# First chunk of an attention and MoE kernel: part of an exponential moved to GpSimd, a cast moved to VectorE, filler products on TensorE, and the order of the weight conversion

## The chip, the cores and the metric

One core of a Trainium2 chip. The metric is device time in microseconds (us) of one execution, the median of several runs. Engines: TensorE (PE in the rows, its weight loads PEld), VectorE (DVE), ScalarE (ACT), GpSimd (POOL), and SyncE (SP), which issues the DMAs.

## What is computed

Eight sequences of 576 tokens, eight heads of 64. Heads 0 to 3 look at a local band, heads 4 to 7 at every 32nd token; the outputs go through a two-layer network with squared ReLU.

```python
def _attn_ref(q, k, v):                 # (8, 8, 576, 64)
    scores = (1.0 / np.sqrt(D)) * np.matmul(q, k.transpose(0, 1, 3, 2))
    rel = pos[:, None] - pos[None, :]
    mask_local = (rel >= 0) & (rel < 32)                                     # heads 0..3
    mask_strided = (rel >= 0) & (pos[None, :] % 32 == pos[:, None] % 32)     # heads 4..7
    scores = np.where(masks, scores, -1e9)
    attn = np.exp(scores - np.max(scores, axis=-1, keepdims=True))
    attn = attn / (np.sum(attn, axis=-1, keepdims=True) + 1e-09)
    return np.matmul(attn, v)

def _moe_ref(x, w_in, w_out):           # x 4608 x 512, w_in 512 x 2048, w_out 2048 x 512
    h = np.maximum(x @ w_in, 0.0)
    return h * h @ w_out
```

The network's weights come in double precision and the products are made from a high and a low part of each operand (hi x hi, hi x lo, lo x hi), kept in the type `F32R`.

## The kernel before, in words

The 4608 tokens are cut into 12 chunks of 384. For each chunk and each of 16 blocks of 128 features, `up` makes 12 products of 128x384 (line 475) and squares the ReLU, and `down` makes 9 products of 128x512 (line 508) into three banks that hold the output. The main loop's step s runs `up(s)` and `down(s-2)`. TensorE works on nearly nothing else, while the other engines prepare the attention of the next chunk.

Only the first chunk has nothing to hide behind. Before its first `up` it needs

- `first[0]` and `first[1]`: the two pairs of local heads, and `late[0]` and `late[1]`: the two pairs of strided heads, all run by the generator `pe_pair`: scores on TensorE (L325), mask and row minimum on VectorE (L330), exponential on ScalarE (L353, four per head with bias and row sum, for the local pairs; for the strided pairs one per head, L356, after a subtraction on GpSimd, L355), row sums and reciprocal on VectorE (L357 to L359), division (L362, on VectorE for local and GpSimd for strided pairs), transposes on TensorE (L368) with copies out of PSUM (L370 on VectorE, L372 on ScalarE), the product with v (L380 local, L391 strided), and the split into high and low part (L395, L396);
- the weights of the first blocks, which `convert` makes from the raw 64-bit numbers: a rescaling on ScalarE (L154, one per block of weights), then for each half a step on ScalarE (L166), one on VectorE (L169), the high part on ScalarE (L172) and the low part on GpSimd (L173). `convert` goes on through the whole first chunk, one block a step.

In the first chunk `up` ends with ReLU on ScalarE (L483), the square on VectorE (L484), the high part `gh` on ScalarE (L488) and the low part `gl` on VectorE (L489). `gh` and `gl` have two buffers each, so those of block j wait for the products of block j-2.

The order on each engine is made by the tile framework: it takes the program's order as priority and lets an instruction go ahead when, by its own plan of the times, it is ready first. `tc.issue_after(i)` holds the instructions of a block behind i on i's engine alone; `behind` does so for a generator, with one instruction for each engine. A queue, once made, runs strictly in its order. `zeros(bank, n)` makes n products of 128x128 that nobody reads (L605); L503 and the tripled L380 of `first[0]` are of this kind too. The main program (L607 to L650) names the order of the prologue: the scores, 45 filler products, the exponentials of `first[0]` and of the first head of `first[1]`, the scores of `late[1]`, `late[0]`'s exponentials, `first[0]`'s transposes, the exponentials of `first[1]`'s second head, its transposes, `late[1]`'s exponentials, two steps of weights, and so on.

Of the kernel before, what the change touches and what calls it, by code (L numbers as in the profile page):

```python
# [11 lines left out]
AF = mybir.ActivationFunctionType  # L12
ALU = mybir.AluOpType
AX = mybir.AxisListType
# [14 lines left out]
QC = 96  # L29
NW = TC // QC  # L30
# [8 lines left out]
NWARM = 60  # L39
# [10 lines left out]
def f32(ap):  # L50
    return ap.bitcast(F32)
# [11 lines left out]
def windows(c):  # L63

    res, at = [], 0
    for b, g in SEGS[c]:
        for qc in (2 * g, 2 * g + 1):
            if res and res[-1][:2] != (b, qc - 1):
                at += STR
            res.append((b, qc, at))  # L70
            at += QC
    return res
# [14 lines left out]
def attn_moe(ctx: ExitStack, tc, qk_l, v_l, qk_d, v_d, qk_p, v_p, f_s, q_s, k_s, v_s, w_in, w_out, masks, eye, out):  # L87
    nc = tc.nc
# [13 lines left out]
    def psum(i, nm):  # L102

        return ps.tile([P, 512], F32, name=nm, tag=f"ps{i}")
# [17 lines left out]
    last = {}  # L122
# [9 lines left out]
    def fetch(k):  # L132

        p, which = order[k]
        src = (w_out if which else w_in)[p].bitcast(U32).rearrange("p (n t) -> p n t", t=2)
        if k < 12:
            raw = wpool.tile([P, 1024, 2], U32, name=f"raw{k}", tag=f"w{k + 8 if k < 8 else k + 4}")
            nc.sync.dma_start(out=raw, in_=src)
            raws[k] = [(raw, slice(0, 1024))]
        else:  # L140
            raws[k] = []
            for i in range(0, 1024, WP):
                raw = spool.tile([P, WP, 2], U32, name=f"raw{k}_{i}", tag="s3", bufs=5)
                nc.sync.dma_start(out=raw, in_=src[:, i : i + WP])
                raws[k].append((raw, slice(i, i + WP)))

    def convert():

        split = None

        def scale(k):
            for raw, _ in raws[k]:

                nc.scalar.activation(f32(raw[:, :, 1]), f32(raw[:, :, 1]), AF.Prelu, scale=2.0**-112, alpha=-(2.0**32))  # L154

        scale(0)
        for k in range(NFT):
            p, which = order[k]
            t = wpool.tile([P, 2, 1024], F32R, name=f"w{which}_{p}", tag=f"w{k}")
            (wo if which else wi)[p] = t[:, 0], t[:, 1]  # L160
            cuts = [(raw[:, i : i + WP], sl.start + i) for raw, sl in raws.pop(k) for i in range(0, sl.stop - sl.start, WP)]
            for raw, at in cuts:

                z = psum(zbank[next(zturn) % len(zbank)], f"z{k}_{at}").bitcast(U32)
                w, hi, lo = raw[:, :, 1], t[:, 0, at : at + WP], t[:, 1, at : at + WP]
                first_step = nc.scalar.activation(z, raw[:, :, 0], AF.Copy, bias=-0.49, scale=2.0**-29 * (1 - 2.0**-9))  # L166
                if split:
                    split()
                last["v"] = nc.vector.scalar_tensor_tensor(out=w, in0=w, scalar=3, in1=z, op0=ALU.logical_shift_left, op1=ALU.bitwise_or)  # L169

                def split(w=w, hi=hi, lo=lo, at=at, k=k):
                    last["a"] = nc.scalar.copy(hi, f32(w))  # L172
                    last["g"] = nc.gpsimd.tensor_sub(lo, f32(w), f32(hi))  # L173
                    if at and 4 <= k < 12:
                        fetch(k + 4)

                if k == 0 and at:
                    split()
                    split = None
                if not at and k + 1 < NFT and k + 1 in raws:  # L180
                    with tc.issue_after(first_step.ins):
                        scale(k + 1)
                yield
        split()
# [110 lines left out]
    def pe_pair(c, pr, local, qk, vr, es, pt, banks, sm, single):  # L295
# [3 lines left out]
        if local:  # L299
            kw, wins, nv = KW, [at for _, _, at in windows(c)], P  # L300
            src, vsrc = qk_d[c, pr], v_d[c, pr]
            mk = [mask_sb[:QC, w % 2, :] for w in range(NW)]
        else:
            kw, wins, nv = QC, [QC * w for w in range(NW)], QC
# [9 lines left out]
        nm = small.tile([P, 2, NW], F32, name=f"nm{u}", tag="nm")  # L314
        rs = small.tile([P, 2, NW], F32, name=f"rs{u}", tag="rs")
        ss = sums[sm]
# [3 lines left out]
        e4 = [blocks(e) for e in es]  # L320

        r4 = [blocks(t) for t in s_ps] if single else e4
# [23 lines left out]
                minima(h, s)  # L346
        yield
        for h in range(2):
            if single:
                for w in range(NW):  # L350
                    if c == 0 and pr and h and not w:
                        yield
                    last["a"] = nc.scalar.activation(r4[h][:, w], e4[h][:, w], AF.Exp, bias=nm[:QC, h, w : w + 1], scale=-1.0, accum_out=ss[:QC, NW * h + w, :1])  # L353
            else:
                nc.gpsimd.tensor_sub(e4[h], e4[h], nm[:QC, h].unsqueeze(2).broadcast_to([QC, NW, kw]))  # L355
                last["a"] = nc.scalar.activation(e4[h], e4[h], AF.Exp, scale=-1.0)  # L356
                nc.vector.tensor_reduce(out=ss[:QC, NW * h : NW * (h + 1), 0], in_=e4[h], op=ALU.add, axis=AX.X)  # L357
        nc.vector.tensor_reduce(out=rs[:QC].rearrange("p h w -> p (h w)"), in_=ss[:QC], op=ALU.add, axis=AX.X)
        last["v"] = nc.vector.reciprocal(rs[:QC], rs[:QC])  # L359
# [4 lines left out]
        p4 = pt.rearrange("p (h w q) -> p h w q", h=2, w=NW)  # L364
        for h in range(2):
            t = s_ps[h] if s_ps else banks()
            for w in range(NW):
                nc.tensor.transpose(t[:kw, w * QC : (w + 1) * QC], e4[h][:, w], ident[:QC, :QC])  # L368
            if c == 0 and not local:
                nc.vector.tensor_copy(pt[:kw, h * TC : (h + 1) * TC], t[:kw, :TC])  # L370
            else:
                last["a"] = nc.scalar.copy(pt[:kw, h * TC : (h + 1) * TC], t[:kw, :TC])  # L372
# [92 lines left out]
    def up(c, j):  # L465
        x = xt[c]
        p, o = divmod(j, 2)
        ph = psum((c * NFT + j) % 3, f"h{c}_{j}")
        n = 0
        for kt in range(4):  # L470
            kind, kk = "ls"[kt // 2], kt % 2
            xh, xl = x[kind, "h"][:, kk, :], x[kind, "l"][:, kk, :]
            wsl = slice(kt * 256 + o * P, kt * 256 + (o + 1) * P)
            for w, xx in ((wi[p][0], xh), (wi[p][0], xl), (wi[p][1], xh)):
                done = nc.tensor.matmul(ph[:, :TC], w[:, wsl], xx, start=n == 0, stop=n == 11)  # L475
                n += 1
        gh = gpool.tile([P, TC], F32R, name=f"gh{c}_{j}", tag="gh")
        gl = gpool.tile([P, TC], F32R, name=f"gl{c}_{j}", tag="gl")
        g = ph[:, :TC]
        if c == 0:  # L480

            r = p_t[j % 2].rearrange("p w q -> p (w q)")
            nc.scalar.activation(r, g, AF.Relu)  # L483
            nc.vector.scalar_tensor_tensor(out=g, in0=g, scalar=0.0, in1=r, op0=ALU.max, op1=ALU.mult)  # L484
        else:
            nc.scalar.activation(g, g, AF.Relu)  # L486
            nc.scalar.activation(g, g, AF.Square)  # L487
        last["gh"] = nc.scalar.copy(gh, g)  # L488
        nc.vector.tensor_sub(gl, g, f32(gh))  # L489
        g_tiles[c, j] = gh, gl  # L490
        return done
# [29 lines left out]
    def behind(ins, gen):  # L521

        while True:
            with ExitStack() as st:
                for i in ins.values():
                    st.enter_context(tc.issue_after(i.ins))
                try:
                    k = next(gen)
                except StopIteration:
                    return  # L530
            yield k
# [47 lines left out]
    def take(c, which):  # L579

        if NPLAIN <= c < NCHUNK:
            for h in map(int, which):
                if (c, h) not in heads:
                    heads[c, h] = pe_head(c, h)
                with ExitStack() as st:
# [4 lines left out]
                    last["pe"] = last.get("mm", last["pe"])  # L590

    ungated = convert()

    late = [pair_at(0, pr, False, 2 + pr, ("y0", "14")[pr]) for pr in range(2)]
# [7 lines left out]
    def zeros(bank, n):  # L602
        w_ps = psum(bank, f"w_ps{bank}")
        for _ in range(n):
            nc.tensor.matmul(w_ps[:, :P], warm, warm, start=True, stop=True)  # L605
# [17 lines left out]
        for k in range(NEARLY, 8):  # L623
            fetch(k)
    next(late[0])
    zeros(1, 3 * NWARM // 4)
    next(first[0])
    parts = last["v"], last["a"]
    with tc.issue_after(parts[1].ins):
# [4 lines left out]
    next(first[0])  # L634
    with tc.issue_after(last["a"].ins):
        next(first[1])
    weights = behind({"a": last["a"]}, ungated)
    next(first[1])
    next(late[1])
    for _ in range(2):  # L640
        next(weights)
    next(first[0])
# [4 lines left out]
    weights = behind({"a": last["a"]}, ungated)  # L647
# [6 lines left out]
    for s in range(NS + 2):  # L654
        c, j = divmod(s, NFT)
# [19 lines left out]
        if s < NFT - 2:  # L675

            weights = behind({"a": last["gh"]} | ({"x": last["xs"]} if s > NFT - 4 else {}), ungated)
# [108 lines left out]
```

## Time and profile before

| what | us |
|---|---|
| median of 3 runs | 880.89 (880.71 to 881.8) |
| the profiled execution | 881.58 |
| its span, first to last instruction | 879.80 |
| TensorE busy in the span | 869.2 |
| ScalarE, VectorE, GpSimd busy | 571.7, 640.5, 672.4 |

All times in the rows are counted from the span's start. The profiled execution took 1.78 us more than its span, and 0.69 us more than the median. TensorE's "busy" is a union of overlapping products: an `up` product is listed with some 0.33 us and a `down` product with 0.39 us, but the next one begins about 0.17 and 0.23 us later.

### The profile page before, as it was taken

The numbers are of one execution on the slowest core, as the hardware profiler recorded it, in microseconds if no ns is written. First come the engines' busy times: TensorE is split into PE (matmuls) and PEld (weight loads), VectorE is DVE, ScalarE is ACT, GpSimd is POOL, SyncE is SP. The second block draws the span as 40 slices with busy tenths as digits, with TensorE's granted clock in tenths as the row PEclk, the third lists the DMA queues.
The fourth block names the chain that finished last, engine by engine and source line by source line (L and its number), as shares of the span: only waits on it lengthen the run. The fifth ranks groups of instructions, "written<-read, shape, count | busy, mean of one in ns | idle before, by whom it ended". The sixth has DMA issues, their size and how long they took to land.

```text
span 879.8 us, 14906 instructions
## 1 busy us (share of the span) xinstructions
PE 869.2 (99%) x4773; PEld 790.0 (90%) x4773; DVE 640.5 (73%) x1900; ACT 571.7 (65%) x1506; POOL 672.4 (76%) x718
## 2 busy tenths in 40 slices
PE   8999999999999999999999999999999999999997
PEld 7788899999999999999999999999998989999996
DVE  5796687787787887878878778878787787883111
ACT  6999777586676566657657758657666665664332
POOL 3589778877988989888988978997998899782000
PEclk9999999999999999999999999999999999999999
DMA  9853531323123023112202302312131121000000
GB/s 356 356 199 107 163 101 39 101 84 113 31 78 111 26 89 103 44 51 85 67 13 80 115 13 74 97 38 75 31 102 57 32 71 61 6 1 12 26 1 36
DMA packets 26798, 71.41 MB, mean 81 GB/s; under 512 B 2976, under 2 KB 8736, under 8 KB 25184
## 3 DMA queue, kind: packets, MB, share of 16 engines
q1 hardware_dynamic: 26432, 70.14, 24.0%
q8 instruction: 37, 0.61, 0.3%
q14 instruction: 41, 0.34, 0.1%
q10 hardware_dynamic: 288, 0.33, 0.1%
HBM read 61.01 MB, written 9.44 MB: 80 GB/s over the span
## 4 chain that ended last, share of the span: by engine, by line
PE 90%; POOL 4%; ACT 2%; DVE 1%; DMA 1%; issue 1%; DVEq 0%; POOLq 0%; ACTq 0%
PE y L508 42%; PE h L475 42%; POOL w L173 2%; PE s L237 2%; PE o L283 2%; DMA raw<-w_out 1%; PE w_ps L605 1%; PE b L380 1%; ACT b L353 1%; ACT raw L154 1%; ACT z L166 0%; POOL pp L447 0%; DVE sc L432 0%; PE b L391 0%; POOL e L355 0%
## 5 line engine op out<-in xcount | busy, mean ns | idle before, releaser
L508 PE MATMUL y<-w,gh 128*128 128x512 f32 x1152 | 357.9, 391 | 0.5 <-POOL w L173 0.5
L508 PEld LDWEIGHTS y<-w,gh 128*128 128x128 f32 x1152 | 212.7, 188 | 40.5 <-POOL w L173 0.8
L475 PE MATMUL h<-xlh,w 128*128 128x384 f32 x768 | 229.1, 339 | 1.4 <-ACT xlh L395 0.9
L447 POOL TENSOR_TENSOR pp<-vs,sc 128x448 f32<-128x448 f32 (+10 forms) x192 | 189.9, 1013 | 48.9 <-DVE qs L448 23.0
L475 PE MATMUL h<-xsh,w 128*128 128x384 f32 x768 | 226.3, 335 | 0.3 <-POOL w L173 0.3
L508 PE MATMUL y<-w,gl 128*128 128x512 f32 x576 | 225.2, 392 | 0.0
L425 POOL TENSOR_TENSOR pq<-ks,qs 128x512 f32<-128x512 f32 (+2 forms) x192 | 197.7, 1050 | 18.6 <-DVE sc L426 13.2
L489 DVE TENSOR_TENSOR gl<-h,gh 128x384 fp32r<-128x384 f32 x192 | 105.5, 550 | 80.9 <-ACT gh L488 79.6
L488 ACT CAST gh<-h 128x384 fp32r<-128x384 f32 x192 | 91.3, 476 | 104.4 <-PE y L508 103.0
L486 ACT ACTIVATE h<-h 128x384 f32<-128x384 f32 x176 | 83.1, 472 | 110.0 <-PE h L475 109.5
L426 DVE TENSOR_REDUCE sc<-pq 128x8 f32<-128x512 f32 (+4 forms) x228 | 119.7, 534 | 45.3 <-POOL pq L425 42.6
L475 PEld LDWEIGHTS h<-xlh,w 128*128 128x128 f32 x768 | 141.3, 188 | 5.0 <-ACT xlh L395 1.1
L475 PEld LDWEIGHTS h<-xsh,w 128*128 128x128 f32 x768 | 141.4, 188 | 1.1 <-POOL w L173 0.6
L475 PE MATMUL h<-xll,w 128*128 128x384 f32 x384 | 129.0, 336 | 0.0
L508 PEld LDWEIGHTS y<-w,gl 128*128 128x128 f32 x576 | 108.1, 188 | 22.9
L475 PE MATMUL h<-xsl,w 128*128 128x384 f32 x384 | 128.3, 334 | 0.0
L448 DVE TENSOR_REDUCE qs<-pp 128x64 f32<-128x448 f32 (+11 forms) x192 | 106.4, 562 | 27.2 <-POOL pp L447 25.2
L487 ACT ACTIVATE h<-h 128x384 f32<-128x384 f32 x176 | 83.2, 473 | 3.6
L262 DVE STREAM_TRANSPOSE p_t<-e 32x128 f32<-32x128 f32 x240 | 72.3, 301 | 11.2 <-ACT e L251 6.6
L475 PEld LDWEIGHTS h<-xll,w 128*128 128x128 f32 x384 | 72.2, 188 | 2.4 <-DVE xll L396 0.3
L475 PEld LDWEIGHTS h<-xsl,w 128*128 128x128 f32 x384 | 72.1, 188 | 0.1
L246 ACT ACTIVATE e<-e,nm 96x128 f32<-96x128 f32 x160 | 62.5, 392 | 10.0 <-DVE nm L229 8.7
(101 smaller groups left out, 1077.2 us busy)
## 6 DMA issues: line engine op xcount, KB each, us to landing
qk<-qk_l SPq DMA_DIRECT2D x24, 400.0 KB, 3.2
y<-ysb SPq DMA_DIRECT2D x36, 256.0 KB, 3.5
raw<-w_in SPq DMA_DIRECT2D x7, 1024.0 KB, 10.9
qk<-qk_l SPq DMA_DIRECT2D x16, 416.0 KB, 3.2
vs<-v_s SPq DMA_DIRECT2D x10, 576.0 KB, 3.8
raw<-w_out SPq DMA_DIRECT2D x5, 1024.0 KB, 12.6
v<-v_l SPq DMA_DIRECT2D x40, 128.0 KB, 2.0
ks<-k_s SPq DMA_DIRECT2D x8, 576.0 KB, 3.7
```

Of the source, the lines that this page charges most:

```text
L246: nc.scalar.activation(e[:QC, cut(w)], e[:QC, cut(w)], AF.Exp, bias=nmax[:QC, w : w + 1], scale=-1.0, accum_out=ssum[:QC, w, :1])
L262: nc.vector.transpose(out=pt[STR * k : STR * (k + 1), :, STR * r : STR * (r + 1)], in_=e.rearrange("p (w k) -> p w k", k=KW)[STR * r : STR ...
L425: nc.gpsimd.tensor_mul(pv, kt[:, a : a + m, :], qt[:, i - i0 : i - i0 + 1, :].broadcast_to([P, m, D]))
L426: nc.vector.tensor_reduce(out=sc[:, i - i0, a : a + m], in_=pv, op=ALU.add, axis=AX.X)
L447: nc.gpsimd.tensor_mul(pv, vt[:, a : a + nd, :n], sc[:, il : il + 1, :n].broadcast_to([P, nd, n]))
L448: nc.vector.tensor_reduce(out=ot[:, il, a : a + nd], in_=pv, op=ALU.add, axis=AX.X)
L475: done = nc.tensor.matmul(ph[:, :TC], w[:, wsl], xx, start=n == 0, stop=n == 11)
L486: nc.scalar.activation(g, g, AF.Relu)
L487: nc.scalar.activation(g, g, AF.Square)
L488: last["gh"] = nc.scalar.copy(gh, g)
L489: nc.vector.tensor_sub(gl, g, f32(gh))
L508: done = nc.tensor.matmul(y_ps[c][t], g[:, sl], w[:, wsl], start=j == 0 and k == 0, stop=j == NFT - 1 and k == 2)
```

## The change

Five edits, all for the first chunk:

1. `first[1]`'s second head: its four exponentials with bias and row sum become a subtraction on GpSimd, one exponential over 96x512 on ScalarE and one row sum on VectorE.
2. More filler on TensorE: `zeros(1, ...)` makes 55 products in place of 45, and the four transposes of `first[0]`'s second head are made twice.
3. `convert` gives up control once more, after its first rescaling, and that first rescaling is called right behind `first[1]`'s exponentials, ahead of `first[1]`'s transposes and `late[1]`'s exponentials.
4. The first two steps of weights are held behind the first exponential of `late[1]` on ScalarE (`last["a0"]`) and behind its reciprocal on VectorE, in place of behind the last exponential of `first[1]` on ScalarE.
5. In `up` of the first chunk ScalarE makes the ReLU twice and no longer makes `gh`; VectorE makes the square twice, first into `gh`, then in place. The weights of a step are held behind the second ReLU, where they were held behind the copy to `gh`.

```diff
@@ convert @@
         scale(0)
+        yield
@@ pe_pair @@
         for h in range(2):
-            if single:
+            if single and pr and h:
+                yield
+                nc.gpsimd.tensor_sub(e4[h], e4[h], nm[:QC, h].unsqueeze(2).broadcast_to([QC, NW, kw]))
+                last["a"] = nc.scalar.activation(r4[h], e4[h], AF.Exp, scale=-1.0)
+                nc.vector.tensor_reduce(out=ss[:QC, NW * h : NW * (h + 1), 0], in_=r4[h], op=ALU.add, axis=AX.X)
+            elif single:
                 for w in range(NW):
-                    if c == 0 and pr and h and not w:
-                        yield
                     last["a"] = nc.scalar.activation(r4[h][:, w], e4[h][:, w], AF.Exp, bias=nm[:QC, h, w : w + 1], scale=-1.0, accum_out=ss[:QC, NW * h + w, :1])
             else:
...
+                last["a0"] = last["a0" if h else "a"]
...
-            for w in range(NW):
+            for w in [*range(NW)] * (2 if c == 0 and local and not pr and h else 1):
                 nc.tensor.transpose(t[:kw, w * QC : (w + 1) * QC], e4[h][:, w], ident[:QC, :QC])
@@ up @@
             nc.scalar.activation(r, g, AF.Relu)
-            nc.vector.scalar_tensor_tensor(out=g, in0=g, scalar=0.0, in1=r, op0=ALU.max, op1=ALU.mult)
+            last["gh"] = nc.scalar.activation(r, g, AF.Relu)
+            for t in (gh, g):
+                nc.vector.scalar_tensor_tensor(out=t, in0=g, scalar=0.0, in1=r, op0=ALU.max, op1=ALU.mult)
         else:
             nc.scalar.activation(g, g, AF.Relu)
             nc.scalar.activation(g, g, AF.Square)
-        last["gh"] = nc.scalar.copy(gh, g)
+            last["gh"] = nc.scalar.copy(gh, g)
@@ the main program @@
-    zeros(1, 3 * NWARM // 4)
+    zeros(1, NWARM - 5)
...
-    weights = behind({"a": last["a"]}, ungated)
+    next(behind({"a": last["a"]}, ungated))
     next(first[1])
     next(late[1])
+    weights = behind({"a": last["a0"], "v": last["v"]}, ungated)
```

## Rows read from the trace of the kernel before

**Rows 1.** The page, first part: busy us, share of the span, instructions.

```profile
PE 869.2 (99%) x4773; PEld 790.0 (90%) x4773; DVE 640.5 (73%) x1900; ACT 571.7 (65%) x1506; POOL 672.4 (76%) x718
```

**Rows 2.** Waits of TensorE, 27.5 to 110 us: waiter <- releaser: total us, times, longest.

```profile
PE h L475 <- ACT xlh L395: 0.9, 1, 0.9
PE s L237 <- POOL qx L223: 0.5, 1, 0.5
PE y L508 <- POOL w L173: 0.5, 1, 0.5
PE h L475 <- ACT w L172: 0.4, 1, 0.4
PE h L475 <- POOL w L173: 0.3, 1, 0.3
```

**Rows 3.** Stretches: length, PE, PEld, DVE, ACT, POOL busy (instructions), clock, DMA, GB/s.

```profile
13.10:16.50 3.40, 2.28 (x26) 1.62 (x25) 3.33 (x18) 3.33 (x14) 1.50 (x3) 1.00 1.01 419
16.50:20.00 3.50, 3.50 (x46) 3.50 (x44) 2.57 (x17) 3.13 (x11) 2.88 (x4) 0.51 1.01 417
20.00:23.40 3.40, 2.94 (x30) 2.20 (x29) 2.70 (x5) 2.91 (x6) 1.61 (x2) 1.00 1.01 412
...
42.00:57.00 15.00, 14.88 (x77) 13.29 (x78) 13.47 (x32) 14.31 (x26) 11.75 (x13) 1.00 0.40 143
```

**Rows 4.** The same for the transposes of L368 alone: length, PE, PEld, clock, DMA.

```profile
20.00:23.40 3.40, 2.54 (x24) 2.03 (x24) 1.00 1.01 412
```

**Rows 5.** TensorE in order of time: start, us, operation, [idle before <- releaser].

```profile
9.86 2.69 PE L605 MATMUL w_ps<-p_t 128*128 128x128 bf16 x45
...
14.42 1.17 PE L368 MATMUL b<-ident,e 96*128 96x96 f32 x8 [0.62 <-ACT b L353]
15.97 4.22 PE L380 MATMUL b<-pt,v 128*64 128x96 f32 x48 [0.38 <-ACT pt L372]
...
27.50 0.45 PE L475 MATMUL h<-xlh,w 128*128 128x384 f32 x1
...
88.03 0.88 PE L380 MATMUL b<-pt,v 128*64 128x96 f32 x16
```

**Rows 6.** ScalarE in order of time.

```profile
15.46 0.83 ACT L372 COPY pt<-b 128x384 f32<-128x384 f32 x2
...
18.77 0.35 ACT L353 ACTIVATE b<-e,nm 96x128 f32<-96x128 f32 x1
19.16 1.11 ACT L154 ACTIVATE raw<-raw 128x1024 f32<-128x1024 f32 x1
...
60.16 0.63 ACT L356 ACTIVATE e<-e 96x512 f32<-96x512 f32 x1
```

**Rows 7.** VectorE in order of time.

```profile
21.17 1.27 DVE L362 TENSOR_TENSOR e<-b,rs 96x512 f32<-96x512 f32 x2
...
61.26 0.67 DVE L357 TENSOR_REDUCE sums<-e 96x4 f32<-96x512 f32 x1
```

**Rows 8.** GpSimd in order of time.

```profile
20.03 1.61 POOL L362 TENSOR_TENSOR w<-w,rs 96x384 f32<-96x384 f32 x2 [0.30 <-DVE rs L359]
24.88 1.30 POOL L173 TENSOR_TENSOR w<-raw,w 128x512 fp32r<-128x512 f32 x1 [3.25 <-ACT w L172]
...
58.08 1.03 POOL L355 TENSOR_TENSOR e<-e,nm 96x512 f32<-96x512 f32 x1
```

**Rows 9.** DMA issues from 6.0 to 6.4 us: KB, us from issue to landing.

```profile
raw<-w_in SPq DMA_DIRECT2D x1, 1024.0 KB, 8.8
```

**Rows 10.** Groups by line, 27 to 108 us: busy us, mean ns | idle before, releasers.

```profile
L484 DVE SCALAR_TENSOR_TENSOR h<-h,p_t 128x384 f32<-128x384 f32 x16 | 9.0, 561 | 5.4 <-ACT p_t L483 5.3
L489 DVE TENSOR_TENSOR gl<-h,gh 128x384 fp32r<-128x384 f32 x16 | 8.8, 547 | 3.1 <-ACT gh L488 3.0
...
L483 ACT ACTIVATE p_t<-h 128x384 f32<-128x384 f32 x16 | 7.7, 479 | 1.1 <-PE h L475 1.1
L488 ACT CAST gh<-h 128x384 fp32r<-128x384 f32 x16 | 7.5, 469 | 1.4 <-PE y L508 0.9 <-DVE h L484 0.4
```

## The prediction

> **What bounds the kernel now.** The page comes first: TensorE is busy for 869.2 of 879.8 us [rows 1], so only its idle time and its slow time can be won. The list of its waits shows where that is: from the first product of `up` at 27.50 us [rows 5] to 110 us there are five waits with 2.6 us in all [rows 2], and behind them the products follow each other without a gap. What is left is the 27.50 us ahead of `up`, and its order of time shows two weak places. Between the scores and the transposes of `first[0]` TensorE is idle for 0.62 us, and 0.38 us more before the 48 products with v [rows 5]. And in the stretch 13.1 to 16.5, where it is busy for 2.28 of 3.40 us, the granted clock is 1.00, but in the next, 16.5 to 20.0, it is 0.51, the lower of its two levels (1.2 and 2.4 GHz) [rows 3]. The 48 products take 4.22 us there, 0.088 us each; at full clock 16 of them take 0.88 us, 0.055 each [rows 5].
>
> **The prologue: the second head of `first[1]`.** Four exponentials, each followed by a read of the row sum, go from ScalarE; the last begins at 18.77 and ends at 19.16, when the rescaling begins, so one takes 0.39 us [rows 6]. They were interleaved with `late[1]`'s. In their place comes one exponential of 96x512, 0.63 us, issued behind the copies of `first[0]` that take 15.46 to 16.29 [rows 6]. Those copies wait for the doubled transposes: four more at 0.11 us (24 take 2.54 [rows 4]) are 0.43 us, of which the first copy covers some 0.2, so the exponential runs from about 16.5 to 17.1. Its input is ready: the subtraction is 1.03 us on GpSimd [rows 8], which has nothing to do before the strided pairs' minima are made, and VectorE makes this head's ahead of them; `late[0]`'s subtractions, queued behind it, come some 0.3 us later, and ScalarE is then still at `first[1]`'s first head, so that costs nothing (0.3 if not). VectorE gets a row sum more, 0.67 us [rows 7], and the work queued behind it there is `late[1]`'s row sums. The division L362 of `first[1]`, which began at 21.17 [rows 7], can begin near 18.6, 2.5 us earlier.
>
> `late[1]` gains nothing. The first rescaling (1.11 us [rows 6]) is now ahead of its exponentials on ScalarE; its data was issued just after 6.0 us and landed 8.8 us later, before 15 [rows 9], so nothing blocks, but `late[1]`'s first exponential moves back by up to that. And `first[1]`'s division (1.27) stands ahead of `late[1]`'s sums on VectorE. Its division on GpSimd, 20.03 to 21.64 [rows 8], moves by -0.3 to +1.2 us; I take +0.8. From its end to the first `up` now go 5.9 us, part of it in TensorE's queue behind the products of `first[1]`, which then are done; the chain itself (transposes, VectorE copies, L391, ScalarE casts) is some 4 us. So `late[1]` lets `up` begin at 22.4 + 3.5 = 25.9, the last products of L391 lying beside the first six of `up`, which need only local heads.
>
> **The prologue: TensorE.** Ten filler products at 2.69 / 45 = 0.06 us [rows 5] push the scores of `late[1]` by 0.6 us, into the 0.62 us wait: nothing. The doubled transposes fill the second gap and start the 48 products at 16.4 in place of 15.97, 0.4 us later. If the clock stays up they take 48 x 0.055 = 2.64 us and end at 19.0, not 20.19: 1.15 us won. From there to 27.50 TensorE has 7.3 us of work and waits, of which 0.6 us or so are waits for `first[1]`'s and `late[0]`'s copies. So `up` could begin between 25.7 (waits gone) and 26.4 (waits kept). With `late[1]`'s 25.9 I take 26.0: **-1.5 us**.
>
> A page speaks against the doubled transposes. The Trainium skill (TensorE: Matmul & The Clock Gate, "Part 4: PE-mode transpose") says that a transpose on TensorE does not count as busy, for the clock, in the way a product does. By that the 48 products would again run at the lower level, and the sum would be near that of the second rival. The trace disagrees: from 20.0 to 23.4 us transposes are 2.54 of TensorE's 2.94 us [rows 3, 4], and the clock stays at 1.00.
>
> **The weights.** The first low part starts at 24.88 on GpSimd [rows 8], 2.6 us before the product at 27.50; `up` needs it by its third product. With the rescaling some 2 us earlier and VectorE's step let go behind `late[1]`'s reciprocal (about 20.5 to 21) both halves come about 2 us earlier, so they do not set the start at 26.0. The next blocks set three of the five waits: 0.5 + 0.4 + 0.3 [rows 2]. ScalarE is full there; it saves 4 x 0.39 - 0.63 = 0.9 us of exponentials, and of its idle time between 16.5 and 23.4 us, 0.9 us [rows 3], some can go. So the conversion moves by 0.9 to 1.8 us, about as much as `up`, and the three waits stay: 0, between +0.4 and -0.6.
>
> **The sixteen steps.** ScalarE: a ReLU (479 ns) for a cast (469) [rows 10]: 16 x 0.01 = 0.2 us, nothing. VectorE: one square more. The write to `gh` in this form is not in the trace; the nearest rows have the same inputs, one from PSUM and one from SBUF, with output to PSUM (561 ns) and to SBUF (547) [rows 10], begun some 0.47 us apart. 16 x 0.47 = 7.5 us. Against it VectorE no longer waits for ScalarE's cast: 3.0 us [rows 10]. Net 4.5 us, over 80 us; in the whole span VectorE is idle for a quarter [rows 1]. The wait of `gh` for the products of two blocks before moves from ScalarE (0.9 us [rows 10]) to VectorE, with the conversion's L169 queued behind. I take 0 for TensorE here; the ends are -1.4 (below) and +4.5 (no cover).
>
> At the end of the chunk TensorE waits 0.9 and 0.5 us [rows 2] for work that VectorE and GpSimd finish last. Some of VectorE's 3.0 us behind the cast [rows 10] lie there; between 0 and the whole 1.4 I take **-0.3 us**.
>
> **Sum.** -1.5 - 0.3 = -1.8 us: the span 879.8 becomes 878.0, this execution 881.58 becomes 879.8, and the median, 0.69 us below that execution, 879.1. A measurement of this kernel tells about 0.2%, 1.76 us, from no change; the forecast is just at that bound.
>
> **Rivals.**
> - More than forecast (15%): with `gh` no longer crossing engines the wait at the chunk's end goes whole, and half of the three early ones: -1.5 - 1.4 - 0.6 = -3.5, 877.4. For it: VectorE's 3.0 us of waits [rows 10] lie in the queue that feeds everything. Against: GpSimd is nearly full later in the chunk, and is given nothing back.
> - The start comes earlier but is swallowed (27%): either the clock falls all the same (10%), or the conversion (17%), whose engines have no room, pins TensorE at the next blocks. With the clock down the 48 products, begun at 16.4, end where they ended or later; what stays is the waits of 0.6 less 0.3: 880.6. The pinned case gives the same: the waits of [rows 2] grow by what the start gained. For it: weights come up to a microsecond ahead of use, no more; against: ScalarE saves 0.9 us at the front.
> - Slower (18%): VectorE becomes the bound. From 42 to 57 us it is busy for 13.47 of 15 us [rows 3]; 3.6 steps at 0.47 add 1.7, which makes 15.2. From there on each step's L169 comes later, and with it the high part and GpSimd's low part, and TensorE waits for weights. It decides when VectorE's net addition (4.5 us) finds no idle time that the others don't need. Price: 4.5 less the 1.8 won, half a microsecond for what is covered: +2.2, 883.1.
> - The edits do what they say in all of these; the framework may order the queues otherwise than I read, which widens each case by half a microsecond.
>
> **How the numbers follow.** Forecast 879.1 with 40%, its own range 878.1 to 880.1. Faster than 879.13: a little over half of it and rival one, a bit from the second: 0.40. Slower than 882.65: 0.16. Same: 0.44. The range 876.9 to 882.7 takes in the forecast, the swallowed case, most of the first rival and the near edge of the slow one.
>
> **What would show it.** Clock at 1.00 from 16.5 to 20 and 48 products in 2.6 us; the first product of `up` near 26.0 in place of 27.50; `first[1]`'s division near 18.6; no wait of VectorE for `gh`; the three early waits for weights unchanged at about 1.2 us. Wrong if the clock is still 0.5 there, if TensorE gains waits for L172 or L173 between 42 and 100 us, if VectorE has no idle time left there, or if the waits after 100 us grow by what the start gained.

## The result, and the profile after

The changed kernel takes 884.58 us (median of 6, 883.02 to 885.84) against 880.80 (6 runs) for the kernel before: ratio 1.0043, 95% interval 1.0033 to 1.0054. It is slower by 3.8 us where 1.8 us less was forecast, and outside the range. The profiled execution took 884.37 us with a span of 882.6. The clock is not what was lost: the four executions with a mean granted clock of 0.999 or 1.000 took 883.85 to 884.79 us.

The page's first part for the changed kernel, which answers [rows 1]: TensorE's busy time is the same, so what was lost is waiting.

```profile
PE 869.2 (98%) x4787; PEld 789.5 (89%) x4787; DVE 647.9 (73%) x1917; ACT 571.2 (65%) x1499; POOL 673.9 (76%) x719
```

The changed kernel's lines bear other numbers: `up` is L482, `down` L517, the division L368, the squares L493, `gl` L498. Stretches as in [rows 3]:

```profile
16.50:20.00 3.50, 2.98 (x53) 2.41 (x52) 3.40 (x18) 3.50 (x7) 3.18 (x4) 1.00 1.02 421
...
42.00:57.00 15.00, 15.00 (x79) 13.32 (x78) 13.65 (x38) 14.97 (x28) 12.46 (x13) 1.00 0.49 152
```

The clock stays at 1.00 from 16.5 to 20 us, where it was 0.51. TensorE in order of time, answering [rows 5]: the 48 products take 0.38 + 2.19 us in place of 4.22, but the first `up` is at 28.12 us in place of 27.50, behind two waits for copies of `late[1]`.

```profile
16.31 0.38 PE L387 MATMUL b<-pt,v 128*64 128x96 f32 x2
16.95 2.19 PE L387 MATMUL b<-pt,v 128*64 128x96 f32 x46 [0.26 <-ACT pt L379]
...
25.76 0.35 PE L398 MATMUL b<-w,v 96*32 96x96 f32 x2 [0.32 <-DVE w L377]
26.68 1.51 PE L398 MATMUL b<-w,v 96*32 96x96 f32 x30 [0.57 <-DVE w L377]
28.12 0.44 PE L482 MATMUL h<-xlh,w 128*128 128x384 f32 x1
```

What made `late[1]` late stands in three queues. ScalarE (b is `first[1]`, w is `late[1]`):

```profile
16.79 0.60 ACT L354 ACTIVATE b<-e 96x512 f32<-96x512 f32 x1
17.32 1.19 ACT L154 ACTIVATE raw<-raw 128x1024 f32<-128x1024 f32 x1
18.39 0.94 ACT L361 ACTIVATE w<-w 96x384 f32<-96x384 f32 x2
```

VectorE: the division of `first[1]` (L368), `late[1]`'s sums (L363), then copies and a split of the other pairs ahead of the last two steps that `late[1]` needs (L364, L365):

```profile
18.58 1.28 DVE L368 TENSOR_TENSOR e<-b,rs 96x512 f32<-96x512 f32 x2
19.78 1.00 DVE L363 TENSOR_REDUCE sums<-w 96x4 f32<-96x384 f32 x2
20.70 1.01 DVE L377 COPY pt<-b 96x384 f32<-96x384 f32 x2
21.63 0.15 DVE L364 TENSOR_REDUCE rs<-sums 96x8 f32<-96x16 f32 x1
21.71 0.54 DVE L403 TENSOR_TENSOR xll<-b,xlh 128x384 fp32r<-128x384 f32 x1
22.17 0.19 DVE L365 RECIPROCAL rs<-rs 96x8 f32<-96x8 f32 x1
```

GpSimd, which had the division of `late[1]` at 20.03 before [rows 8]:

```profile
22.50 1.61 POOL L368 TENSOR_TENSOR w<-w,rs 96x384 f32<-96x384 f32 x2 [2.62 <-DVE rs L365]
```

The loss at the first `up` is 0.6 us; at the first product of the third chunk it is 2.6 (176.49 against 173.90). The 2.0 us between are all lost before TensorE's product L238, which waits for `qx`: it begins at 110.56 us, 82.4 behind the first `up`, where the same product L237 of the kernel before begins at 107.92, 80.4 behind. From there to the end of the span it is 772.0 us against 771.9. That is 2.8 us between the two spans; the medians differ by 3.8, since the kernel before was profiled in one of its slower executions (881.58 us). TensorE's waits from 27.5 to 112 us make 4.2 us, against 2.6 in [rows 2]; the old wait for `xlh` and three for weights are gone or smaller, new ones are `gh`, `gl` and `xll`, and the wait for `qx` grew from 0.5:

```profile
PE s L238 <- POOL qx L224: 1.5, 1, 1.5
PE y L517 <- DVE gh L493: 1.0, 1, 1.0
PE b L375 <- DVE xll L403: 0.6, 1, 0.6
PE y L517 <- DVE gl L498: 0.6, 1, 0.6
PE y L517 <- POOL w L174: 0.5, 1, 0.5
```

Groups from 27 to 108 us, answering [rows 10]: the square to `gh` takes 548 ns, and VectorE's wait of 3.0 us for ScalarE's cast is gone (0.1 us before `gl`).

```profile
L493 DVE SCALAR_TENSOR_TENSOR h<-h,p_t 128x384 f32<-128x384 f32 x16 | 8.8, 553 | 0.0
L493 DVE SCALAR_TENSOR_TENSOR gh<-h,p_t 128x384 fp32r<-128x384 f32 x16 | 8.8, 548 | 1.1 <-ACT p_t L491 0.9
L498 DVE TENSOR_TENSOR gl<-h,gh 128x384 fp32r<-128x384 f32 x16 | 8.7, 548 | 0.1
...
L490 ACT ACTIVATE p_t<-h 128x384 f32<-128x384 f32 x16 | 7.8, 488 | 1.4 <-PE h L482 1.4
```

The waits for `gh` and `gl` stand at the first `down`, where the buffers are still free. There the second ReLU (L491) of block 0 comes 1.9 us behind the first (L490) on ScalarE, and `gh` waits for it; `gl` then waits on VectorE behind two steps of the weights. ScalarE, VectorE and TensorE:

```profile
33.95 0.49 ACT L490 ACTIVATE p_t<-h 128x384 f32<-128x384 f32 x1
...
35.85 0.47 ACT L491 ACTIVATE p_t<-h 128x384 f32<-128x384 f32 x1
```

```profile
36.35 0.56 DVE L493 SCALAR_TENSOR_TENSOR gh<-h,p_t 128x384 fp32r<-128x384 f32 x1 [0.67 <-ACT p_t L491]
```

```profile
36.96 1.66 PE L517 MATMUL y<-w,gh 128*128 128x512 f32 x6 [0.97 <-DVE gh L493]
```

One more line stands out. VectorE's subtraction L439, which takes 0.55 us at its second place in the kernel before, took 3.84 us here; at its first place it is the other way about, 3.29 us at 47.07 us before and 0.72 us at 46.92 us here. First VectorE, then GpSimd, late in the chunk:

```profile
89.47 3.84 DVE L439 TENSOR_TENSOR sc<-sc,mx 128x36 f32<-128x36 f32 x1
93.23 0.55 DVE L403 TENSOR_TENSOR xll<-b,xlh 128x384 fp32r<-128x384 f32 x1
```

```profile
88.12 5.13 POOL L174 TENSOR_TENSOR w<-raw,w 128x512 fp32r<-128x512 f32 x4
```

It ends when GpSimd's four low parts end, and `xll`, for which TensorE waits 0.6 us, is queued behind it.

### The profile page after: what moved, and what is told of

Its sections match the earlier page's. It is cut to its first block, busy times and chain, and to the rows that moved or that the text cites. A ratio compares the mean times of both kernels' runs of the same rounds, so it can differ in the third digit from the quotient of the medians.

```text
span 882.6 us, 14941 instructions
## 1 busy us (share of the span) xinstructions
PE 869.2 (98%) x4787; PEld 789.5 (89%) x4787; DVE 647.9 (73%) x1917; ACT 571.2 (65%) x1499; POOL 673.9 (76%) x719
## 4 chain that ended last, share of the span: by engine, by line
PE 94%; ACT 2%; DVE 2%; POOL 1%; issue 1%; DVEq 0%; POOLq 0%; ACTq 0%
PE h L482 44%; PE y L517 44%; PE s L238 2%; PE o L284 2%; PE w_ps L614 1%; PE b L326 1%; ACT b L358 1%; ACT z L167 1%; DVE sc L439 0%; ACT w L173 0%; PE b L398 0%; DVE raw L170 0%; ACT raw L154 0%; PE b L375 0%; ACT p_t L490 0%
## 5 line engine op out<-in xcount | busy, mean ns | idle before, releaser
L517 PE MATMUL y<-w,gh 128*128 128x512 f32 x1152 | 356.8, 391 | 1.6 <-DVE gh L493 1.0
L517 PEld LDWEIGHTS y<-w,gh 128*128 128x128 f32 x1152 | 212.5, 188 | 42.4 <-POOL w L174 1.2
L482 PE MATMUL h<-xlh,w 128*128 128x384 f32 x768 | 228.7, 338 | 0.0
L482 PE MATMUL h<-xsh,w 128*128 128x384 f32 x768 | 226.2, 335 | 0.1
L517 PE MATMUL y<-w,gl 128*128 128x512 f32 x576 | 223.8, 392 | 0.6 <-DVE gl L498 0.6
L498 DVE TENSOR_TENSOR gl<-h,gh 128x384 fp32r<-128x384 f32 x192 | 105.4, 549 | 82.1 <-ACT gh L497 80.8
L497 ACT CAST gh<-h 128x384 fp32r<-128x384 f32 x176 | 83.9, 476 | 104.8 <-PE y L517 103.7
L482 PEld LDWEIGHTS h<-xlh,w 128*128 128x128 f32 x768 | 141.4, 188 | 3.2 <-POOL w L174 0.4
L482 PEld LDWEIGHTS h<-xsh,w 128*128 128x128 f32 x768 | 141.2, 188 | 0.6 <-POOL w L174 0.4
L517 PEld LDWEIGHTS y<-w,gl 128*128 128x128 f32 x576 | 108.0, 188 | 23.8 <-DVE gl L498 1.0
L482 PE MATMUL h<-xll,w 128*128 128x384 f32 x384 | 129.0, 336 | 0.0
L482 PE MATMUL h<-xsl,w 128*128 128x384 f32 x384 | 128.3, 334 | 0.0
L482 PEld LDWEIGHTS h<-xll,w 128*128 128x128 f32 x384 | 72.2, 188 | 2.2
L482 PEld LDWEIGHTS h<-xsl,w 128*128 128x128 f32 x384 | 72.1, 188 | 0.0
```

Of the source, the lines that this page charges most:

```text
L517: done = nc.tensor.matmul(y_ps[c][t], g[:, sl], w[:, wsl], start=j == 0 and k == 0, stop=j == NFT - 1 and k == 2)
```

## The experiments

Medians; the ratio's 95% interval is against the kernel before on the same chip (its medians there: 880.64 to 880.90).

| run | us | ratio |
|---|---|---|
| e1: before + edit 5 | 882.34 | 1.0013 to 1.0032 |
| e2: changed, edit 5 undone | 882.89 | 1.0019 to 1.0038 |
| e3: changed, one ReLU | 884.49 | 1.0029 to 1.0059 |
| e4: changed, edits 3 and 4 undone | 884.29 | 1.0024 to 1.0054 |
| e5: before + edit 1 | 882.28 | 1.0009 to 1.0030 |
| e6: before + edit 2 | 880.05 | 0.9986 to 1.0006 |
| e7: before + edits 3, 4 | 882.27 | 1.0010 to 1.0028 |
| e8: changed, one subtraction on GpSimd | 886.45 | 1.0058 to 1.0088 |
| e9: before + 1, 2, `late[1]` first, held | 884.41 | 1.0021 to 1.0052 |
| e10: before + a square of no use | 881.17 | 0.9995 to 1.0021 |
| e11: e9 without the hold | 883.46 | 1.0018 to 1.0039 |
| e12: e11 + edit 5 | 885.56 | 1.0023 to 1.0058 |
| f1: before + 2, 5 | 881.49 | 0.9998 to 1.0016 |
| f2: before + 2 + a square of no use | 880.46 | 0.9987 to 1.0016 |
| f3: before + 2, weights held behind ReLU | 880.75 | 0.9992 to 1.0011 |
| f4: before + 2, cast on VectorE | 879.85 | 0.9979 to 0.9998 |
| f5: before + 2, 5 with one ReLU | 882.09 | 1.0008 to 1.0027 |
| f6: changed, f4's form in place of edit 5 | 881.47 | 1.0001 to 1.0019 |

**The edits one by one: e1, e5, e6, e7, and e2.** Each takes its edits from the diff, word for word.

> The kernel before with edit 5 alone (two ReLUs on ScalarE, two squares on VectorE, no cast). Theory A, the steps cost: VectorE's 16 more squares and the late second ReLU make gh late and the end of the chunk late; the first product of up stays at 27.5 us, the second chunk's first up comes 1.5 to 3 us later, median 882.5 to 884. Theory B, the prologue costs and all else is carried along: within 0.7 us of before, 880.3 to 881.5.

> The changed kernel with edit 5 taken back: edits 1 to 4 alone. Theory A: the first product of up stays near 28.1 us, 0.6 later than before, the rest of the chunk goes as before, median 881 to 882. Theory B: the delay of the second strided pair's division (22.5 against 20.0 us) pushes the whole chunk, median 883.5 to 885.

> The kernel before with edit 1 alone (second head of the second local pair by a GpSimd subtraction and one exponential). If the local pair's earlier division, now ahead of the strided pair's row sums on VectorE, is what delays that pair: its division begins 8 us or more behind the first local division (6.4 in the kernel before), up starts no earlier, 881.5 to 883. If edit 1 does what I forecast: division at 6.4 to 7.5, up 1 us earlier, 879.5 to 880.6.

> The kernel before with edit 2 alone (55 filler products, four transposes twice). If filler only keeps the clock up: 1.00 throughout the prologue, the first up about 12.9 us behind the first local division in place of 13.9, 879.8 to 880.8. If it costs: the later minima of the last strided pair push its division beyond 7 us behind the first local division, 881.5 to 882.5.

> The kernel before with edits 3 and 4 alone (first rescaling early, the first weights behind the strided pair's reciprocal). If the rescaling ahead of the strided pair's exponentials is the cost: that pair's division begins 7.4 us or more behind the first local division and the time is 881.5 to 883. If not: 6.4 to 6.8, and 880 to 881.

Against the kernel before on the same chip (880.64 for e1 to e4, 880.79 for e5 to e8) the edits alone give +1.5 (edit 1), -0.7 (edit 2), +1.5 (edits 3 and 4) and +1.7 (edit 5): together +3.9 before rounding, where the whole gave +3.8. Edit 2's -0.7 lies within the noise, since its interval takes in 1. Edits 1 to 4 together (e2) give +2.3 (882.89, between its two expected ranges), which is what their own add to; e1, at 882.34, lies just under its Theory A, and e5 and e7 in the ranges in which the edit costs. Edits 1, 3 with 4, and 5 each cost on their own, and no single one is the cause. The sum does not hold everywhere: e4, below, has edits 1, 2 and 5, which add to +2.5, and it gave +3.7 (interval 2.1 to 4.8, four executions).

The filler does to the clock and the start what was forecast. In e6 the stretch has the clock at 1.00 and the first `up` begins at 26.55:

```profile
16.50:20.00 3.50, 3.21 (x55) 2.53 (x52) 2.40 (x18) 3.00 (x12) 3.02 (x4) 1.00 1.02 419
```

```profile
26.55 0.44 PE L475 MATMUL h<-xlh,w 128*128 128x384 f32 x1
```

Edit 1 alone does not leave `late[1]` where it was. ScalarE in e5:

```profile
16.55 0.60 ACT L353 ACTIVATE b<-e 96x512 f32<-96x512 f32 x1
17.08 1.14 ACT L154 ACTIVATE raw<-raw 128x1024 f32<-128x1024 f32 x1
18.11 0.63 ACT L166 ACTIVATE z<-raw 128x512 uint32<-128x512 uint32 x1
18.66 1.15 ACT L154 ACTIVATE raw<-raw 128x1024 f32<-128x1024 f32 x1
19.70 0.93 ACT L360 ACTIVATE w<-w 96x384 f32<-96x384 f32 x2
```

The weights are held behind `first[1]`'s last exponential, which now ends at 17.1 us in place of 19.2; so 2.6 us of weights (17.08 to 19.70) go ahead of `late[1]`'s exponentials, and its division on GpSimd begins at 24.73 in place of 20.03. TensorE begins `up` with the local heads at 25.19, but the strided half of the features comes late and block 3 starts at 37.19, after 35.45 before. In e7 the same hold, moved behind `late[1]` while `first[1]` keeps its four exponentials, pushes the last of these behind a step and a rescaling of the weights: the local division moves from 21.17 to 22.0 us, and that of `late[1]` from 20.03 to 22.19. So each of these edits shifts the order of a queue that other chains pass through.

**The old order of the weights, and the strided pair first: e4, e9, e11, e12.** e4 undoes edits 3 and 4 in the changed kernel. e9 and e11 are the kernel before with edits 1 and 2, and `late[1]`'s exponentials go ahead of `first[1]`'s second head; in e9, shown here, the local division is also held behind `late[1]`'s reciprocal, which e11 leaves out; e12 is e11 with edit 5.

```diff
+                last["a0"] = last["a0" if h else "a"]
...
-    with tc.issue_after(last["a"].ins):
+    copied = last["a"]
+    next(late[1])
+    exps = last["a0"], last["a"]
+    with tc.issue_after(copied.ins), tc.issue_after(last["v"].ins):
         next(first[1])
-    weights = behind({"a": last["a"]}, ungated)
+    weights = behind({"a": last["a"], "b": exps[0], "c": exps[1]}, ungated)
     next(first[1])
-    next(late[1])
```

> The changed kernel with edits 3 and 4 taken back: the first rescaling again behind the second strided pair's exponentials. If the rescaling is what delays that pair (1.07 us ahead of its exponentials on ScalarE), its division begins near 21.4 in place of 22.5 and the first product of up comes near 27.1 in place of 28.1; theory B then gives 883 to 884, theory A the same 1 us at most. If it is VectorE's order (row sums behind the local pair's division), both stay: 22.5 and 28.1, and 884 to 885.

> The kernel before with edits 1 and 2, with the last strided pair's exponentials called ahead of the second local pair's, the weights held behind both of them on ScalarE, and the local pair's row sum and division held behind the strided pair's reciprocal on VectorE. Queue theory (the strided pair is last, and what is helped ahead of it only takes its turn): its division begins 6.4 to 7 us behind the first local division (9.1 in the changed kernel), first up 11.5 to 12.5 us behind it with no wait for strided heads after, 878 to 880. If TensorE or the weights bound the prologue instead: no better than the filler alone, 880 or more.

> The same without the hold on VectorE: the local pair's division is free to go ahead of the strided pair's reciprocal. Queue theory: 6.4 to 7.5, 878 to 880; against the run before it this tells what the local pair's place on VectorE alone is worth (up to 0.7 us either way).

> The kernel of the second run of this set (strided pair first) with edit 5: two ReLUs, two squares. If the costs of prologue and steps add up: 1.7 us over that run, so 880 to 882; if the late prologue of the changed kernel is what makes edit 5 dear: within 0.7 us of that run.

In e4 the weights go ahead of `late[1]` as in e5 (its division at 24.72 us): the old order of the weights behind the new exponential is no better (884.29), though `up` begins at 26.23 us: the time is that of its second case, the positions of neither. In e9 and e11 the expected 2 us at `late[1]` were had, and brought nothing. In e11 its division begins at 20.47 us, the local one at 21.50, and `up` at 27.98: GpSimd, VectorE and TensorE, one line each.

```profile
20.47 1.61 POOL L367 TENSOR_TENSOR w<-w,rs 96x384 f32<-96x384 f32 x2
```

```profile
21.50 1.28 DVE L367 TENSOR_TENSOR e<-b,rs 96x512 f32<-96x512 f32 x2
```

```profile
27.98 0.44 PE L480 MATMUL h<-xlh,w 128*128 128x384 f32 x1 [0.17 <-DVE xsl L401]
```

What `late[1]` wins, the local pair loses on the same VectorE, and both go through TensorE before `up`. In e9 (local division at 24.63) a wait of 1.35 us ahead of the local products at 29.02 was followed by a clock of 0.57 from 30.5 to 34.5 us, and e12 shows 0.58 and 0.57 from 21 to 29 us. In e11 the mean clock over the span was 0.995 or 0.996 in eight executions, which took 882.8 us or more, and 0.999 in two, which took 880.94 and 881.43, one of them the profiled one. e12 is 2.1 us over e11, but its two executions with a clock of 1.000 (881.41 and 882.00) are only 0.5 us above those two on average, so how much of the 2.1 is the clock stays open. So the theory that the two queues were in the wrong order explains the late division, but correcting the order gains nothing; that part of it fell.

**The second ReLU and the clash: e3, e8.** e3 drops the first of the two ReLUs; e8 puts the subtraction L439 of the second chunk on GpSimd.

```diff
-            nc.scalar.activation(r, g, AF.Relu)
             last["gh"] = nc.scalar.activation(r, g, AF.Relu)
...
-            nc.vector.tensor_sub(s, s, mx[:, :ni].unsqueeze(2).broadcast_to([P, ni, i1]))
+            (nc.gpsimd if c == 1 else nc.vector).tensor_sub(s, s, mx[:, :ni].unsqueeze(2).broadcast_to([P, ni, i1]))
```

> The changed kernel with one ReLU in place of two. Theory A in the form that the second ReLU does it (it is placed up to 3.6 us behind the first on ScalarE, and gh waits for it): 880.5 to 882, and up(3) no longer comes behind down(0). Theory A in the form that VectorE's added squares do it: no gain, 884 to 885. Theory B: no more than 1 us of gain, 883.5 to 885.

> The changed kernel with the second chunk's subtraction of the row maximum (128x36, two inputs in SBUF, 3.84 us on VectorE at 89.5 us) on GpSimd in place of VectorE. If VectorE's wait for GpSimd there is what makes the end of the chunk late: the second chunk's first up comes 2 to 3 us earlier, 881.5 to 883. If the chunk is late for another reason, and the lock only lies beside it: 884 to 885.

ScalarE with 7.8 us less work changes nothing (884.49), so its load does not bound. e8 is slower than the changed kernel (ratio 1.0073 against 1.0043): the subtraction then queues on GpSimd behind the same four low parts (it starts at 93.19 us), and freeing VectorE gave nothing back. Nor does the time follow the clash in other traces: at its second place the subtraction takes 0.19 us in e3's profiled execution, of 883.48 us, and 4.87 us in e1's, of 881.38. The clash is thus not shown to be the changed kernel's loss.

**Why edit 5 costs: e10, f1 to f6.** e10 and f2 add a square into `gl`, later overwritten, so that VectorE has edit 5's load and ScalarE keeps the cast (first diff). f3 only moves the hold of the weights to the ReLU (the first two lines of the second diff). f4 also makes the cast on VectorE, in place of a second square (the whole second diff); f6 is that form in the changed kernel. f1 is edit 5 itself, and f5 is edit 5 with e3's one ReLU.

```diff
+            nc.vector.scalar_tensor_tensor(out=gl, in0=g, scalar=0.0, in1=r, op0=ALU.max, op1=ALU.mult)
             nc.vector.scalar_tensor_tensor(out=g, in0=g, scalar=0.0, in1=r, op0=ALU.max, op1=ALU.mult)
```

```diff
-            nc.scalar.activation(r, g, AF.Relu)
+            last["gh"] = nc.scalar.activation(r, g, AF.Relu)
             nc.vector.scalar_tensor_tensor(out=g, in0=g, scalar=0.0, in1=r, op0=ALU.max, op1=ALU.mult)
+            nc.vector.tensor_copy(gh, g)
...
-        last["gh"] = nc.scalar.copy(gh, g)
+            last["gh"] = nc.scalar.copy(gh, g)
```

> The kernel before with one useless square more per step of the first chunk on VectorE (into gl, which is overwritten), the cast left on ScalarE. If VectorE's load is the cost of edit 5 (1.7 us alone): 882 to 883. If it is the cast's move and the order that follows from it: 880.3 to 881.5.

> Kernel before with edits 2 and 5. The filler keeps TensorE's clock up, so that a clock that falls in one execution and not in another no longer blurs the comparison with e6_filler_only (880.05). Theory A: edit 5 has a cost of its own in the chunk (order of the work behind ReLU), 1.7 us as in e1_square_only: about 881.7, with more time between the first product of up of block 0 and the start of the third chunk than the 145.8 us of e6_filler_only, 147.0 or more. Rival: what e1_square_only lost was clock, and the edit is free: 880.1 and 145.8 us.

> Kernel before with edit 2 and, on VectorE, one more square per block of the first chunk whose result is overwritten; the cast to gh stays on ScalarE. Theory A (VectorE has room; the cost of edit 5 is in what gh now waits for): 880.1 to 880.4. Rival (VectorE's load of 7.5 us is the cost): 881.7, as with edit 5.

> Kernel before with edit 2; nothing moves, but the weights of a step are held behind ScalarE's ReLU and no longer behind its cast to gh, as edit 5 holds them behind its second ReLU. Theory A1 (the earlier hold lets conversion go ahead of gh on ScalarE and VectorE, so that down waits for gh and gl): 881 to 882, with new waits of down for gh or gl. Rival A2 (the hold is not it; gh and gl one behind the other on VectorE are): 880.1, no such waits.

> Kernel before with edit 2; VectorE makes one square and then the cast to gh, ScalarE one ReLU and nothing more, weights held behind that ReLU. ScalarE has 7.5 us less work in the chunk. Theory A2 (gh and gl on one engine, behind its other work, cost the time): 881 to 882, although ScalarE is relieved. Rival (the time of edit 5 is ScalarE's second ReLU, which takes the place of the cast): 880 or less.

> Kernel before with edit 2 and edit 5 without its second ReLU: VectorE writes the square to gh and then in place, ScalarE makes one ReLU, weights held behind it. It stands between f1_filler_square (881.49: two ReLUs, two squares) and f4_filler_cast_on_vector (879.85: one ReLU, a square and a cast on VectorE). If the second ReLU on ScalarE costs the 1.4 us of f1_filler_square over e6_filler_only, this gives about 879.9. If the second square on VectorE in place of a cast does, about 881.5.

> The changed kernel with the form of f4_filler_cast_on_vector: one ReLU on ScalarE, one square and then the cast to gh on VectorE, weights held behind the ReLU. If that form is free behind the changed prologue too, it gives what e2_prologue_only gives without edit 5, 882.9 or less. If the order that the changed prologue brings costs the rest of edit 5, it stays near 884.5, as e3_one_relu did.

Load alone costs nothing that can be told in the medians (e10 +0.4 over the kernel before, f2 +0.4 over e6), though two of e10's ten executions took more than 883 us and three of f2's 884.0 or more. The hold moved alone gives +0.7 over e6, and edit 5 itself +1.4 (f1), both with intervals that overlap e6's. f1's executions fall into two groups, five of 880.5 to 881.0 us and five of 882.0 to 882.3, and its trace is of the faster. But f4 and f5 differ by 2.2 us with intervals apart, and f6 takes 3.1 us from the changed kernel and 3.0 from e3, from which it differs in this form alone, again apart. They have the same number of VectorE instructions of the same length; VectorE's groups from 25.5 to 108 us, f4 and then f5:

```profile
L484 DVE SCALAR_TENSOR_TENSOR h<-h,p_t 128x384 f32<-128x384 f32 x16 | 8.9, 559 | 2.8 <-ACT p_t L483 2.7
L485 DVE CAST gh<-h 128x384 fp32r<-128x384 f32 x16 | 8.8, 548 | 0.2 <-PE y L509 0.2
```

```profile
L485 DVE SCALAR_TENSOR_TENSOR h<-h,p_t 128x384 f32<-128x384 f32 x16 | 8.9, 554 | 0.0
L485 DVE SCALAR_TENSOR_TENSOR gh<-h,p_t 128x384 fp32r<-128x384 f32 x16 | 8.8, 552 | 2.2 <-PE y L509 1.7 <-ACT p_t L483 0.4
```

With the cast, the square in place runs while TensorE still reads the old `gh`, and the wait for TensorE is 0.2 us in all. With `gh` written first, that wait stands ahead of all three instructions and is 1.7 us. The changed kernel, with its second ReLU, is not like that: of VectorE's 1.1 us ahead of `gh`, 0.9 are for that ReLU. TensorE pays at the chunk's end; its waits from 27 to 110 us, f4 and then f5:

```profile
PE h L475 <- POOL w L173: 1.2, 3, 0.8
PE h L475 <- ACT xlh L395: 0.6, 1, 0.6
```

```profile
PE s L237 <- POOL qx L223: 1.4, 1, 1.4
PE h L475 <- POOL w L173: 1.3, 3, 0.8
PE h L475 <- ACT xlh L395: 0.6, 1, 0.6
PE b L380 <- ACT pt L372: 0.6, 1, 0.6
```

The new waits for `qx` and `pt`, 2.0 us, are nearly the whole difference. From the first `up` to the product that waits for `qx`, f4 takes 79.5 us and f5 81.7, e6 and f6 79.8, e3 82.3 and the changed kernel 82.4: with the cast the chunk costs no more than in e6, and what f6 has over e6 is its prologue. That the second square in place of a cast costs the time is shown, in both prologues. That it does so through the wait for `gh`'s buffer is not shown: the rows of f5 fit it, those of the changed kernel do not, and the two orders also let the framework place the next chunk's work otherwise. f4, at 879.85 us (0.9979 to 0.9998), is the best of all kernels here, and ahead of both; against e6 it is no different.

## Why the prediction was wrong, by its steps

- **The filler and the clock: right.** Clock 1.00, and 0.38 + 2.19 us for the 48 products (2.64 forecast). Its worth was sized from one execution in which the clock fell. Of 114 executions of the kernel before in these comparisons, 28 have a mean granted clock of 0.999 or 1.000 over the span, with a median of 879.65 us, and 86 one of 0.997 or 0.998, with 880.90. In e6 nine of ten have 0.999 or 1.000. By this, keeping the clock up is worth 1.3 us, and only in those where it falls; e6's median is 0.7 lower, within the noise. The filler also has a price that was put at nothing: in e6 `late[1]`'s division begins 7.0 us behind the first local division, in the kernel before 6.4.
- **`first[1]`'s division: right.** 18.58 us, near 18.6 forecast.
- **`late[1]`'s division: the step that failed first.** It was given -0.3 to +1.2, and took +2.5 (22.50 for 20.03). Priced were a rescaling on ScalarE and the local division on VectorE; by the end of `late[1]`'s sums that had cost 1.3 us (20.78 for 19.45), about the upper end given. Not priced were `late[0]`'s copies L377 (1.01 us) and the split L403 (0.54) of `first[0]`, which stood behind `late[1]`'s reciprocal before and now stand ahead of it: 1.1 us more. From the division's end to the first `up` it took 4.0 us, as the chain was read (some 4), not the 3.5 taken. Start: 26.0 forecast, 28.12 measured. That the late division alone makes the start late is not shown: in e11 it was back at 20.47, and `up` began at 27.98.
- **The weights: neutral within the bundle.** Taking edits 3 and 4 out of the changed kernel gains nothing (e4, 884.29); alone they cost 1.5 us (e7), by what they do to the other queues. The changed kernel's waits for weights are 0.5 us in all, below the forecast's 1.2.
- **The sixteen steps: the second that failed.** 0 was taken (between -1.4 and +4.5), since VectorE has idle time; e1 measured +1.7, and in the changed kernel f6's form, with a cast in place of the second square and the same load on VectorE, is 3.1 us better. The duration (0.55 us), the end of the wait for the cast and ScalarE's neutrality (e3) were right. So what failed is that load and idle time were taken to decide, and the order of the steps was priced at nothing. What the trace shows in its place are TensorE's waits of 1.6 us for `gh` and `gl` and those for `qx` and `xll`. The wait for `gh`'s buffer, which the prediction saw moving to VectorE, is not what makes the first two; by which path the second square makes the chunk late stays open.
- **The end of the chunk: wrong sign.** -0.3 forecast; the waits there went from 1.4 us (0.9 + 0.5) to 2.1 (1.5 for `qx`, 0.6 for `xll`).
- **The rivals.** The slow side was right in sign, with +2.2 us (883.1) for the +3.8 measured, but its mechanism fell, so that much was luck: VectorE was to have no idle time left from 42 to 57 us, and it was busy for 13.65 of 15 us; load alone (e10, f2) costs nothing that the medians tell. The swallowed start came true in no form: the clock stayed up, and conversion did not pin TensorE. The rule of the Trainium skill weighed there (TensorE: Matmul & The Clock Gate, "Part 4: PE-mode transpose") would have had the clock low; the measured clock is 1.00. Which of the ten products and the four transposes held it was not tried apart.

## What to carry to other kernels

Where a few microseconds of start-up pass through strictly ordered queues, price an edit by what it puts ahead of the last-needed instruction on each queue, including small work of others that becomes ready earlier; making one of two parallel chains early can delay the other on the engine that they share. Equal load does not mean equal time: square then cast was 2.2 us better than two squares of the same length. That a step which waits for a buffer should come behind those with a free output is a guess from f4 and f5, worth a run and not shown here. Test the edits of a bundle alone before reading the bundle: here three of four parts cost 1.5 to 1.7 us each, and the gain of the fourth was within the noise.

## What the runs showed of the hardware

VectorE's subtraction with both inputs in SBUF can wait through several GpSimd instructions that follow each other, not just for the one that is under way. The sharpest case is f2's profiled execution, with 884.01 us one of three among ten above 884.0, where the others took 879.9 to 880.7. VectorE, GpSimd, TensorE, and the stretch with its clock:

```profile
85.31 3.65 DVE L432 TENSOR_TENSOR sc<-sc,mx 128x36 f32<-128x36 f32 x1
88.88 0.55 DVE L396 TENSOR_TENSOR xll<-b,xlh 128x384 fp32r<-128x384 f32 x1
```

```profile
85.08 3.82 POOL L173 TENSOR_TENSOR w<-raw,w 128x512 fp32r<-128x512 f32 x3
```

```profile
89.57 0.52 PE L368 MATMUL b<-ident,e 96*128 96x96 f32 x4 [2.37 <-DVE xll L396]
```

```profile
90.00:94.00 4.00, 4.00 (x14) 3.23 (x13) 2.32 (x9) 2.37 (x5) 1.95 (x3) 0.57 0.71 235
```

A step that takes 0.18 us in f5, with no GpSimd instruction beside it, takes 3.65 us here and ends when GpSimd's three low parts end; `xll` behind it is late, TensorE idles 2.37 us, and then works at a clock of 0.57 for 4 us. The Trainium skill (SBUF — State Buffer, "Who interferes with whom") says that such an instruction and a GpSimd instruction that reads SBUF contend for ports under an exclusive lock, and that the order of issue decides which one waits. The trace agrees that one shuts the other out. VectorE did not get its turn between two GpSimd instructions here, nor in the kernel before at 47.07 us (3.29 us, three low parts) or in e1 (4.87 us); it did in e10 (1.50 us, between the second and the third of three low parts) and in f1 (1.93 us, between two divisions). What decides this is not shown. Whether the other two executions near 884 us met the same was not seen: they have no trace.
